# Moving an angle computation into the main loop, and spreading one row by DMA instead of by a matmul

## The chip, the cores and the metric

The kernel runs on one core of one Trainium2 chip. The metric is the device time of one execution in microseconds (us). In what follows TensorE is called PE in the lines of the profile, its weight loads PEld, VectorE is DVE, ScalarE is ACT, GpSimd is POOL and SyncE is SP. An engine name with a q behind it (SPq) is the queue or sequencer of that engine.

## The reference, cut to what matters

```python
x: (8, 3008, 256)                       # float32
X = real(fft(fft(x, axis=1), axis=2))   # (8*3008, 256) rows
g   = X @ w_gate                        # w_gate, w_val: (256, 1536)
val = X @ w_val
out = (silu(g) * val) @ w_out           # w_out: (1536, 256), float32
```

The kernel folds the 256-point transform over the columns into the weights, and does the 3008-point transform with a table of sines and cosines. The rows of one image come in pairs (row k and row M - k) that are a sum and a difference of the same two parts, P and Q. So one set of matmuls serves two rows: "hp" is the result for the plus row, "hm" for the minus row.

## The kernel before

The work runs over 24 tiles of up to 512 row pairs, and each tile over 12 blocks f of 128 hidden columns. One pair (tile, f) is called a unit, so there are 288 units; "unit 2.4" is tile 2, f = 4, and "unit 24" is unit 2.0. A unit has part_a (the plus rows) and, one unit later, part_b (the minus rows, by adding a correction matmul to the same PSUM buffer). Between them stand the output matmuls of the previous tile ("o<-Wo,hp" and "o<-Wo,hm"), four at a time.

The kernel keeps eight PSUM buffers, shared out as 3 + 3 + 2.

```python
psG = tile_pool(name="psG", bufs=3, space=PSUM)   # g
psV = tile_pool(name="psV", bufs=3, space=PSUM)   # v, and e, o of split units
psO = tile_pool(name="psO", bufs=2, space=PSUM)   # outputs
```

From tile 2 on, six of the twelve units of a tile (nine in tiles 21 and 22, none in the last tile) are "split": their value part is not completed in PSUM but as e and o, two PSUM buffers, so that VectorE makes vv from them and GpSimd does the last product. A split unit needs the row d = 0 of Q on all partitions, as "bc". The kernel before makes bc at the first unit of each tile with a matmul against sel (a matrix with ones in its row 0), followed by a ScalarE copy:

```python
SPLIT = (0, 2, 3, 5, 7, 9)
...
def part_a(u):
    ...
    g = psG.tile([P, T], F32, name="g")
    mm(g, Wp, 0, Pt, True, False)
    mm(g, Wq, 0, Qt, False, True)
    if split(u):
        e = psV.tile([P, T], F32, name="v")
        mm(e, Wp, 1, Pt, True, True)
        o = psV.tile([P, T], F32, name="v")
        mm(o, Wm, 1, Qt, True, True)
        sg = ...silu(g)                                             # ScalarE
        stt(es, bc[t], w0[:, f:f + 1], e, mult, add)                # VectorE
        stt(vp, o, -0.5, es, ...); stt(vm, o, 0.5, es, ...)         # VectorE
        nc.gpsimd.tensor_tensor(hts[t][0][:, f], sg, vp, op=mult)   # GpSimd: hp
        return
    v = psV.tile([P, T], F32, name="v")
    ...                                  # two matmuls; ScalarE sg; VectorE hp
def part_b(u):
    ...    # g += Wm.Q (and v += Wm.Q); ScalarE sg; hm on GpSimd (split) or VectorE
...
for i, u in enumerate(units):
    t, f = u
    if f == 0 and split((t, SPLIT[0])):
        ps = psG.tile([P, T], F32, name="g")
        nc.tensor.matmul(ps[:, :w], sel, pq_tiles(t)[1][:, :w], start=True, stop=True)
        bc[t] = bcp.tile([P, T], F32, name="bc")
        nc.scalar.copy(bc[t][:, :w], ps[:, :w])
    for fn in before.pop(i, ()):
        fn()
    run_loads(3)                   # up to three loads of the next image, on the SP queue
    part_a(u)
    if owork:
        owork.run(4)               # four output matmuls of the tile before
    part_b(prev)
    ...
    if owork and not (prev[1] == nF - 1):
        owork.run(4)
    ...                            # fold steps of the next images on GpSimd, transforms on TensorE
```

Before the loop, and while it runs tile 0, the kernel still builds the odd entries 4i + 1 of the sine table. Their angles (four VectorE instructions) stand in front of the loop; their magnitudes, sines and cosines are hung on units 3 to 8 of tile 0 by the table "before". The "fold" of an image is a chain of GpSimd adds (SDf, EOf, Af, then CE and BB) over loaded rows: XA holds rows of one image ("A"), XC rows of two images ("C").

## Time and profile before

| what | value | view |
|---|---|---|
| time | 700.44 us median of 4 runs, 700.24 to 701.84 | the times |
| span of the profiled run, mean granted clock | 698.6 us, 0.987 | cores |
| TensorE, GpSimd, VectorE, ScalarE busy | 97%, 85%, 74%, 62% | part 1 of the page |
| TensorE in the chain that ended last | 83% | part 4 of the page |
| 21 sel matmuls, 21 ScalarE copies | starts 0.216 us apart; 12.3 us | trace; groups |

The page first. Its part 1 gives the busy time of each engine, its part 2 cuts the span into 40 slices of 17.5 us and shows the busy share (and the granted TensorE clock) of each in tenths. Lines of the page of the kernel before:

```profile
PE 679.1 (97%) x4369; PEld 415.5 (59%) x4369; DVE 519.6 (74%) x925; ACT 433.9 (62%) x765; POOL 593.8 (85%) x577
...
PE   7879989999999999999999999999999999999997
...
POOL 7896999899999999999998989998899655658930
PEclk9979999999999999999999999999999999999999
```

TensorE is full from slice 7 (105 us) on; before, the clock falls (the 7 in the third slice). GpSimd is nearly as full from 70 us to about 540 us.

The groups of instructions show what the change takes away. The columns are line, engine, operation, output and input with shapes, count, then busy us and mean ns of one, then the idle time in front. Two lines of the kernel before:

```profile
L857 ACT COPY bc<-g 128x512 f32<-128x512 f32 (+1 forms) x21 | 12.3, 586 | 5.4 <-PE g L854 5.4
...
L854 PE MATMUL g<-Qt,sel 128*128 128x512 bf16 (+1 forms) x21 | 7.9, 378 | 0.0
```

The mean of 378 ns is not what a matmul costs: the ends of matmuls are modelled, and two in a row start 0.216 us apart at 512 columns. That agrees with the Trainium skill, "TensorE: Matmul & The Clock Gate", section "Wait — 56ns, not 53.3ns?", which gives N over 2.4 GHz plus about 2.5 ns, 215.7 ns at 512 columns. I use this spacing below: a wait of TensorE is the distance of two matmul starts less N/2.4 + 2.5 ns.

The start of the loop, from the timeline of the kernel before. The columns are start and length in us, engine, line, operation, output and input, and in brackets the idle time of that engine before it and what ended it:

```profile
27.12 3.00 DVE L305 SCALAR_TENSOR_TENSOR XA<-XA,mM 128x376 f32<-128x376 f32 x4
...
30.28 0.57 ACT L744 ACTIVATE sg<-g 128x480 f32<-128x480 f32 x1 [4.07 <-DMA XC<-in_x_dram]
...
30.90 0.36 PE L754 MATMUL g<-Qt,Wm 128*128 128x480 bf16 x1 [1.68 <-ACT sg L744]
...
39.62 4.67 POOL L152 TENSOR_TENSOR SDf<-XC 64x1024 f32<-64x1024 f32 x2
...
42.56 2.14 DVE L309 TENSOR_SCALAR XA<-XA 128x752 int32<-128x752 int32 x1
...
44.73 0.92 ACT L315 ACTIVATE Tab<-XA,halfpi 128x752 bf16<-128x752 f32 x1 [2.92 <-DVE XA L309]
...
46.16 0.56 PE L754 MATMUL g<-Qt,Wm 128*128 128x480 bf16 x1 [2.95 <-ACT sg L744]
...
47.28 0.75 DVE L309 TENSOR_SCALAR XA<-XA 128x752 int32<-128x752 int32 x1
```

There are two stalls of TensorE. The first silu (30.28) comes only after the four angle instructions of VectorE (27.12 to 30.12), and TensorE waits 1.68 us for it. (The bracket names a DMA.) At unit 7, the magnitude takes 2.14 us where its second half, at 47.28, takes 0.75 us. It overlaps a pair of GpSimd adds (4.67 us together) and ends 0.41 us after them. The Trainium skill, "SBUF — State Buffer", section "Who interferes with whom", says that a VectorE tensor_scalar in a two-port mode and a GpSimd instruction share a port pair, and that the one which issues second is blocked. The cosine and the next silu stand behind the magnitude, and TensorE waits 2.95 us. In the trace the TensorE clock is half for 3.4 us after the first of these stalls and for 10.2 us after the second.

The third stall is at tile 2, where the first folds must be done. From the timeline of the kernel before:

```profile
69.78 4.67 POOL L152 TENSOR_TENSOR SDf<-XA 128x1024 f32<-128x1024 f32 x2 [6.13 <-DMA XC<-in_x_dram]
...
95.39 2.35 POOL L152 TENSOR_TENSOR SDf<-XC 128x1024 f32<-128x1024 f32 x1 [1.32 <-DMA XA<-in_x_dram]
...
103.29 0.38 PE L717 MATMUL v<-Pt,Wp 128*128 128x512 bf16 x1 [2.39 <-DVE vv L736]
```

GpSimd waits 6.13 us for the loads of image 1 (69.78) and 1.32 us for the next ones (95.39). (The brackets name a load of the other buffer; since the adds read XA and XC, I take the waits to be for their own loads.) It then does the products hp and hm of the split units late, VectorE's vv waits for them, and TensorE waits 2.39 us for vv. Half clock follows for 3.4 us.

Last, the first unit of a later tile, 4.0, in the same view of the kernel before:

```profile
145.67 0.57 ACT L762 ACTIVATE sg<-g 128x480 f32<-128x480 f32 x1 [0.47 <-PE g L754]
...
146.11 0.38 PE L854 MATMUL g<-Qt,sel 128*128 128x512 bf16 x1
...
146.27 0.66 DVE L763 TENSOR_TENSOR hm<-sg,v 128x480 bf16<-128x480 f32 x1 [0.39 <-PE o L677]
...
146.75 0.38 PE L717 MATMUL v<-Pt,Wp 128*128 128x512 bf16 x1
...
146.98 0.38 PE L717 MATMUL v<-Qt,Wm 128*128 128x512 bf16 x1
```

The sel matmul is the one at 146.11. The matmul at 146.98 is that of o (v<-Qt,Wm).

### The profile page before, as it was taken

The page shows a single profiled execution, that of the slowest core. Times are in us where ns is not written, and L with a number is a line of the kernel's source. Part 1 is how long each engine was busy: PE and PEld are TensorE (multiplying, and loading weights), DVE is VectorE, ACT ScalarE, POOL GpSimd, SP SyncE. Part 2 cuts the span into 40 slices and gives each one's busy share as a digit, 9 for nine tenths or more (in the row PEclk, how much of TensorE's full clock was granted, in tenths as well). Part 3 has the DMA queues.
Part 4 walks back from the last instruction along what each step waited for, and adds up shares of the span by engine and source line. Part 5 has one row for each costly group of instructions (what it writes and reads, how often), then busy time and mean ns, then how long its engine had stood idle before and what let it go on. Part 6 is the DMA issues. An engine that isn't in the chain of part 4 may idle for free.

```text
span 698.6 us, 13274 instructions
## 1 busy us (share of the span) xinstructions
PE 679.1 (97%) x4369; PEld 415.5 (59%) x4369; DVE 519.6 (74%) x925; ACT 433.9 (62%) x765; POOL 593.8 (85%) x577
## 2 busy tenths in 40 slices
PE   7879989999999999999999999999999999999997
PEld 4335655566565566565665656655666556656676
DVE  8776667777777778677777777777777777788862
ACT  7465655566565666565665666656666566656663
POOL 7896999899999999999998989998899655658930
PEclk9979999999999999999999999999999999999999
DMA  9636353241612412316125111117111011111112
GB/s 216 112 46 132 107 136 93 63 121 44 160 32 65 132 46 71 111 46 160 34 65 138 39 34 43 46 38 152 37 47 46 31 31 46 45 31 46 46 46 69
DMA packets 45567, 52.55 MB, mean 75 GB/s; under 512 B 6290, under 2 KB 33466, under 8 KB 45498
## 3 DMA queue, kind: packets, MB, share of 16 engines
q1 hardware_dynamic: 42314, 49.35, 26.0%
q0 software_dynamic: 3184, 2.36, 2.5%
q8 instruction: 34, 0.56, 0.3%
q14 instruction: 35, 0.29, 0.1%
HBM read 29.39 MB, written 24.65 MB: 77 GB/s over the span
## 4 chain that ended last, share of the span: by engine, by line
PE 83%; DMA 4%; DVE 4%; issue 4%; POOL 2%; ACT 1%; SPq 1%; ACTq 0%; POOLq 0%; DVEq 0%
PE o L677 32%; PE v L717 16%; PE g L717 15%; PE g L754 8%; PE v L754 4%; PE g L566 3%; PE v L566 3%; DVE vv L736 2%; DMA XC<-in_x_dram 2%; DMA XC_107<-in_x_dram 1%; DMA XA<-in_x_dram 1%; POOL hm L759 1%; DVE vv L734 1%; POOL hp L737 1%; PE g L854 1%
## 5 line engine op out<-in xcount | busy, mean ns | idle before, releaser
L737 POOL TENSOR_TENSOR hp<-sgv,vv 128x512 bf16<-128x512 f32 (+1 forms) x132 | 168.2, 1276 | 49.9 <-DVE vv L734 39.0
L759 POOL TENSOR_TENSOR hm<-sgv,vv 128x512 bf16<-128x512 f32 (+1 forms) x132 | 167.7, 1275 | 8.5 <-ACT sgv L758 8.1
L677 PE MATMUL o<-Wo,hm 128*128 128x256 bf16 (+2 forms) x1140 | 170.5, 273 | 0.0
L677 PE MATMUL o<-Wo,hp 128*128 128x256 bf16 (+2 forms) x1140 | 169.6, 273 | 0.0
L677 PEld LDWEIGHTS <-hp 128*128 128x128 bf16 (+2 forms) x1140 | 111.9, 98 | 68.1 <-issue 8.2
L677 PEld LDWEIGHTS <-hm 128*128 128x128 bf16 (+2 forms) x1140 | 112.2, 99 | 65.8 <-issue 6.6
L732 DVE SCALAR_TENSOR_TENSOR es<-bc,w_85,v 128x512 f32<-128x512 f32 (+1 forms) x132 | 98.1, 743 | 53.0 <-PE v L717 52.8
L745 DVE TENSOR_TENSOR hp<-sg,v 128x512 bf16<-128x512 f32 (+2 forms) x156 | 103.7, 665 | 36.7 <-ACT sg L744 35.9
L744 ACT ACTIVATE sg<-g 128x512 f32<-128x512 f32 (+2 forms) x156 | 90.8, 582 | 45.9 <-PE g L717 41.0
L762 ACT ACTIVATE sg<-g 128x512 f32<-128x512 f32 (+2 forms) x156 | 91.1, 584 | 44.4 <-PE g L754 44.2
L763 DVE TENSOR_TENSOR hm<-sg,v 128x512 bf16<-128x512 f32 (+2 forms) x156 | 103.2, 661 | 19.0 <-ACT sg L762 8.9
L754 PE MATMUL g<-Qt,Wm 128*128 128x512 bf16 (+2 forms) x288 | 108.8, 378 | 5.2 <-ACT sg L744 5.1
L717 PE MATMUL v<-Pt,Wp 128*128 128x512 bf16 (+2 forms) x288 | 108.6, 377 | 2.4 <-DVE vv L736 2.4
L758 ACT ACTIVATE sgv<-g 128x512 f32<-128x512 f32 (+1 forms) x132 | 78.9, 598 | 50.1 <-PE g L754 41.3
L717 PE MATMUL g<-Qt,Wq 128*128 128x512 bf16 (+2 forms) x288 | 108.6, 377 | 0.5 <-DVE Qt L579 0.5
L717 PE MATMUL g<-Pt,Wp 128*128 128x512 bf16 (+2 forms) x288 | 108.8, 378 | 0.1
L729 ACT ACTIVATE sgv<-g 128x512 f32<-128x512 f32 (+1 forms) x132 | 78.7, 596 | 45.0 <-PE g L717 35.9
L734 DVE SCALAR_TENSOR_TENSOR vv<-v,es 128x512 f32<-128x512 f32 (+1 forms) x132 | 91.1, 690 | 19.7 <-POOL hp L737 1.7
L736 DVE SCALAR_TENSOR_TENSOR vv<-v,es 128x512 f32<-128x512 f32 (+1 forms) x132 | 89.7, 680 | 6.2 <-POOL hm L759 3.3
L717 PEld LDWEIGHTS <-Wp 128*128 128x128 bf16 x576 | 56.6, 98 | 42.1 <-issue 5.8
L152 POOL TENSOR_TENSOR SDf<-XA 128x1024 f32<-128x1024 f32 x28 | 66.1, 2365 | 8.0 <-DMA XC<-in_x_dram 6.1
L683 ACT COPY ev<-o 128x512 f32<-128x512 f32 x90 | 52.8, 587 | 30.6 <-PE o L677 29.6
(173 smaller groups left out, 742.2 us busy)
## 6 DMA issues: line engine op xcount, KB each, us to landing
out_dram<-ev SPq DMA_DIRECT2D x96, 128.0 KB
XA<-in_x_dram SPq DMA_DIRECT2D x32, 256.0 KB
XA<-in_x_dram SPq DMA_DIRECT2D x112, 64.0 KB
XC<-in_x_dram SPq DMA_DIRECT2D x105, 32.0 KB
XC<-in_x_dram SPq DMA_DIRECT2D x28, 120.0 KB
out_dram<-ev SPq DMA_DIRECT2D x12, 120.0 KB
out_dram<-ev SPq DMA_DIRECT2D x10, 112.0 KB
XA<-in_x_dram SPq DMA_DIRECT2D x1, 1024.0 KB
```

Of the source, the lines that this page charges most:

```text
L677: nc.tensor.matmul(ps[:n, j, :], hts[minus][:, f, c:c + n], Wo[:, f, :], start=(f == 0), stop=(f == nF - 1))
L717: nc.tensor.matmul(ps[:, :w], Wt[:, gv, fs], src[:, :w], start=start, stop=stop, skip_group_check=True)
L732: stt(es[:, :w], bc[t][:, :w], w0[:, f:f + 1], e[:, :w], op0=Alu.mult, op1=Alu.add)
L734: stt(vp[:, :w], o[:, :w], -0.5, es[:, :w], op0=Alu.mult, op1=Alu.add)
L736: stt(vm[:, w - 1::-1], o[:, :w], 0.5, es[:, :w], op0=Alu.mult, op1=Alu.add)
L737: nc.gpsimd.tensor_tensor(hts[t][0][:, f, :w], sg[:, :w], vp[:, :w], op=Alu.mult)
L744: nc.scalar.activation(sg[:, :w], g[:, :w], AF.Silu)
L745: nc.vector.tensor_tensor(hts[t][0][:, f, :w], sg[:, :w], v[:, :w], op=Alu.mult)
L754: nc.tensor.matmul(ps[:, :w], Wm[:, gv, f * P:(f + 1) * P], Qt[:, :w], start=False, stop=True, skip_group_check=True)
L759: nc.gpsimd.tensor_tensor(hts[t][1][:, f, :w], sg[:, :w], v[:, :w], op=Alu.mult)
L762: nc.scalar.activation(sg[:, :w], g[:, :w], AF.Silu)
L763: nc.vector.tensor_tensor(hts[t][1][:, f, w - 1::-1], sg[:, :w], v[:, :w], op=Alu.mult)
```

## The change

The intent is to take the start of the loop off VectorE's four angle instructions, to put VectorE's work for the 4i + 1 entries where it overlaps no large GpSimd add, and to free TensorE and ScalarE of the sel matmul and its copy: two small DMAs write row 0 of the next tile's Q to DRAM and read it back to all partitions, five units before it is needed (two units for tile 3).

```diff
+    mM = const.tile([P, 4], F32, name="mM")        # was in a pool that closes before the loop
-    mm_, mM = col("mm", 4), col("mM", 4)
+    mm_ = col("mm", 4)
...
-    for ch in range(2):
-        angles(rrO[:, ch], kfO, ch, rrO[:, ch].bitcast(I32))    # in front of the loop
...
+    rowd = tc.dram_tile([nT, T], BF16, name="rowd")
...
-    spread(("C", 1), 14, 1, 12)
-    spread(("A", 1), 14, 13, 24)
+    spread(("C", 1), 14, 6, 14)
+    spread(("A", 1), 14, 15, 24)
...
-    before = {1: weight_unit(1, 0), 2: weight_unit(1, 1),
-              3: [lambda: sine(0, ...)], 4: weight_unit(2, 0), 5: [lambda: sine(1, ...)],
-              6: weight_unit(2, 1) + [lambda: cosines(0)], 7: [lambda: cosines(1)],
-              8: [lambda: weigh(NOO, NTAB)], 9: [lambda: value_rows((1, 2))]}
+    raO = SDf...                                    # the magnitudes go to SDf
+    before = {0: angles_o(0), 1: weight_unit(1, 0), 2: weight_unit(1, 1),
+              3: angles_o(1) + cosine_o(0), 4: weight_unit(2, 0) + cosine_o(1),
+              5: weight_unit(2, 1), 7: sine_o(0), 8: sine_o(1),
+              9: [lambda: weigh(NOO, NTAB), lambda: value_rows((1, 2))]}
...
-        if f == 0 and split((t, SPLIT[0])):
-            ps = psG.tile([P, T], F32, name="g")
-            nc.tensor.matmul(ps[:, :w], sel, pq_tiles(t)[1][:, :w], start=True, stop=True)
-            bc[t] = bcp.tile([P, T], F32, name="bc")
-            nc.scalar.copy(bc[t][:, :w], ps[:, :w])
+        if f == (10 if t == 2 else 7) and t + 1 < nT and split((t + 1, SPLIT[0])):
+            bc[t + 1] = bcp.tile([P, T], BF16, name="bc")
+            nc.sync.dma_start(out=rowd[t + 1:t + 2, :w], in_=pq_tiles(t + 1)[1][0:1, :w])
+            nc.sync.dma_start(out=bc[t + 1][:, :w], in_=rowd[t + 1:t + 2, :w].to_broadcast([P, w]))
```

Here angles_o(ch) is the two angle instructions of one half and its magnitude. The table mM had been in a pool whose space the loop's pools take over, so in the kernel before the first silu waited for the last reader of mM; in the changed one mM stays.

More of the change, by code (lines that the diff above doesn't have):

```diff
@@ L362 @@
     nc.vector.memset(Tab[:, :, :, :, NOO - 1:NOO], 0.0)
-    nc.vector.memset(sel[0:1, :], 1.0)
     vts(m2, pcol, scalar1=0.0, scalar2=-2.0, op0=Alu.not_equal, op1=Alu.mult)
@@ L828, in weights, with angles_o, cosine_o, sine_o @@
         transform_w(fc, gv, k, psO.tile([P, T], F32, name="o"))()
-    def cosines(ch):
-        magnitude(rrO[:, ch], rrO[:, ch])
-        cosine(ch, NOO, NTAB, rrO[:, ch])
     def weight_unit(fc, gv):
         return [lambda k=k: weights(fc, gv, k) for k in range(2)]
-    before = {1: weight_unit(1, 0), 2: weight_unit(1, 1),
-              3: [lambda: sine(0, NOO, NTAB, rrO[:, 0])],
-              4: weight_unit(2, 0),
-              5: [lambda: sine(1, NOO, NTAB, rrO[:, 1])],
-              6: weight_unit(2, 1) + [lambda: cosines(0)],
-              7: [lambda: cosines(1)],
-              8: [lambda: weigh(NOO, NTAB)],
-              9: [lambda: value_rows((1, 2))]}
+    raO = SDf.rearrange("p k a d -> p (k a d)")[:, 0:4 * G].rearrange("p (c q n) -> p c q n", c=2, q=2)
+    def angles_o(ch):
+        return [lambda: angles(rrO[:, ch], kfO, ch, rrO[:, ch].bitcast(I32)),
+                lambda: magnitude(raO[:, ch], rrO[:, ch])]
+    def cosine_o(ch):
+        return [lambda: cosine(ch, NOO, NTAB, raO[:, ch])]
+    def sine_o(ch):
+        return [lambda: sine(ch, NOO, NTAB, rrO[:, ch])]
+    before = {0: angles_o(0), 1: weight_unit(1, 0), 2: weight_unit(1, 1), 3: angles_o(1) + cosine_o(0),
+              4: weight_unit(2, 0) + cosine_o(1), 5: weight_unit(2, 1), 7: sine_o(0), 8: sine_o(1),
+              9: [lambda: weigh(NOO, NTAB), lambda: value_rows((1, 2))]}
     loads = []
@@ L850 @@
         t, f = u
-        if f == 0 and split((t, SPLIT[0])):
-            ps = psG.tile([P, T], F32, name="g")
-            w = width(t)
-            nc.tensor.matmul(ps[:, :w], sel, pq_tiles(t)[1][:, :w], start=True, stop=True)
-            bc.pop(t - 2, None)
-            bc[t] = bcp.tile([P, T], F32, name="bc")
-            nc.scalar.copy(bc[t][:, :w], ps[:, :w])
+        if f == (10 if t == 2 else 7) and t + 1 < nT and split((t + 1, SPLIT[0])):
+            bc.pop(t - 1, None)
+            bc[t + 1] = bcp.tile([P, T], BF16, name="bc")
+            w = width(t + 1)
+            nc.sync.dma_start(out=rowd[t + 1:t + 2, :w], in_=pq_tiles(t + 1)[1][0:1, :w])
+            nc.sync.dma_start(out=bc[t + 1][:, :w], in_=rowd[t + 1:t + 2, :w].to_broadcast([P, w]))
         for fn in before.pop(i, ()):
```

## The prediction

> **What bounds it now.** TensorE: 97% busy by the first part of the page, 83% of the chain that ended last. It loses time only early. By the windows it is busy 13.80 of 17.50 us in 34.9–52.4, 17.24 of 20.0 in 87–107, then 99–100% to 600 us. Its longest waits: for sg (2.9 us) and for vv (2.4). The timeline shows three stalls:
>
> - 29.2–30.9: the first sg starts only at 30.28, as it waits for the four angle instructions on VectorE (27.12–30.12), whose mM column lies in the closed pool.
> - 43.2–46.2: the magnitude of 752 elements takes 2.14 us, ending just after GpSimd's 4.67 us SDf pair (the second takes 0.75 us); cosine (0.92) and sg queue behind it.
> - 100.9–103.3: GpSimd is late with hp: it waited for the image loads of the A fold (6.1 us idle, until 69.78), then for the next C loads (until 95.39).
>
> After each stall the clock falls to half: 3.4, 10.2, 3.4 us, so 8.5 us of TensorE work lost where it is the limit. The Trainium skill ("TensorE: Matmul & The Clock Gate", Part 1) has a 3413 ns activity window; the stretches are one and three of these.
>
> **Removed.** 21 sel matmuls (spacing 0.216 us, 4.5 us of TensorE) and 21 ScalarE copies (0.59 us, 12.4 us, but ScalarE is 62% busy and off the path). The first sg no longer waits for VectorE. The second stall's chain disappears.
>
> **Moved.** VectorE's angles and magnitudes (3.0 + 1.5 us unblocked) stay, half in front of hp of unit 0, half in front of unit 3. From 27 us to the value rows of unit 9 VectorE still has about 17 us (hp/hm 0.63 us each, Wp copies 0.62), so it, not TensorE (13.2 us), sets that stage. The first stall shrinks by 0 to 1 us only; the second is replaced by a smaller one at unit 3. The value rows should be reached near 45.5 instead of 50.53; by unit 24 TensorE is about 7 us ahead.
>
> **Given back.** GpSimd does not follow. The A loads can start 5 us earlier, but the last two now stand behind the first output stores: about 67 instead of 69.8. The C loads of the next images come later in the queue, plus about 2 us for the second small DMA waiting for the first: about 93 instead of 95.4. SP issues are almost back to back there. So GpSimd's hp/hm shift by only 2 to 3 us, and the stall at tile 2 grows from 2.4 to about 7 us. Net of the start: about -2.5 us.
>
> **Added.** Two small DMAs per tile, off the path if they land within five units (10.8 us); at tile 3 only two units are left, perhaps 1 us.
>
> **Sum.** -2.5 (start) -4.0 (20 later sel matmuls; GpSimd, 97–99% busy in 140–300, takes a little) = about -6.5: 694 us, range 688.5 to 698.5.
>
> **Signs.** Value rows near 45–46; no 10 us half-clock stretch; A's first SDf near 67, C's near 93; longest TensorE wait at tile 2 for vv, over 4 us in sum, with a half-clock window behind; 99% TensorE after 110 us.
>
> **What would make it wrong.** If the loads land much earlier, GpSimd follows and the gain is 10–13 us. If the SP queue is held up more by the DMA pair, C folds slip and little remains. If GpSimd saturates, the 4 us are lost too.
>
> Faster by over 2%: 0.06; within 2%: 0.92; slower: 0.02.

## The result and the profile after

The changed kernel took 696.59 us (median of 4 runs, 694.98 to 697.36) against 700.44 us before. The ratio is 0.9938 with a 95% interval of 0.9914 to 0.9962: within 2%, and a real gain of a little over half a per cent. Ratios here and below are the mean time of one kernel's fast runs over the mean of the other's fast runs of the same rounds, so they are not quite the ratio of the medians that I quote beside them. The profiled runs have spans of 698.6 us (clock 0.987) and 694.1 us (clock 0.995).

The page of the changed kernel, the same lines:

```profile
PE 672.0 (97%) x4348; PEld 412.0 (59%) x4348; DVE 519.0 (75%) x924; ACT 423.2 (61%) x744; POOL 593.3 (85%) x577
...
PE   7999969999999999999999999999999999999997
...
POOL 8898999899999899999998989998899655658920
PEclk9999989999999999999999999999999999999999
```

TensorE is shown busy for 7.1 us less, the third slice is whole, but slice 6 (87 to 104 us) has fallen from 8 to 6, and the clock dips there instead. Where the time went is seen best by when the first g matmul of a unit starts, read from both traces:

| unit | before | after | difference |
|---|---|---|---|
| 0.0 | 25.87 | 25.85 | 0.0 |
| 0.2 | 33.62 | 31.25 | -2.4 |
| 0.7 | 42.24 | 40.89 | -1.4 |
| 0.9 | 51.01 | 44.07 | -6.9 |
| 1.0 | 59.69 | 51.00 | -8.7 |
| 2.4 | 93.98 | 85.29 | -8.7 |
| 2.7 | 100.31 | 96.84 | -3.5 |
| 3.0 | 118.51 | 114.74 | -3.8 |
| 10.0 | 310.88 | 307.44 | -3.4 |
| 20.0 | 586.62 | 582.80 | -3.8 |
| 22.0 | 640.86 | 636.50 | -4.4 |
| 23.11 | 684.36 | 680.00 | -4.4 |

So three things happened: tile 0 gained 8.7 us; tile 2 took 5.2 us of it back between units 2.4 and 2.7; and over the nineteen tiles from 3.0 to 22.0 the change gained only 0.6 us (522.35 us before, 521.76 us after), although nineteen sel matmuls of 0.216 us, 4.1 us of work, are gone from that stretch.

The start, timeline of the changed kernel:

```profile
27.10 1.12 DVE L306 SCALAR_TENSOR_TENSOR XA<-XA,mM 128x376 f32<-128x376 f32 x2
...
27.28 0.57 ACT L743 ACTIVATE sg<-g 128x480 f32<-128x480 f32 x1 [1.09 <-DMA XC<-in_x_dram]
...
28.25 1.32 DVE L310 TENSOR_SCALAR SDf<-XA 128x752 int32<-128x752 int32 x1
...
30.19 0.36 PE L753 MATMUL v<-Qt,Wm 128*128 128x480 bf16 x1 [0.79 <-DVE hp L744]
...
35.54 0.72 DVE L310 TENSOR_SCALAR SDf<-XA 128x752 int32<-128x752 int32 x1
...
36.29 0.93 ACT L316 ACTIVATE Tab<-SDf,halfpi 128x752 bf16<-128x752 f32 x1 [0.53 <-DVE SDf L310]
...
36.86 0.36 PE L753 MATMUL v<-Qt,Wm 128*128 128x480 bf16 x1 [0.79 <-DVE hp L744]
...
41.52 4.67 POOL L153 TENSOR_TENSOR SDf<-XC 64x1024 f32<-64x1024 f32 x2
...
43.67 0.54 PE L450 MATMUL o<-SDt,XA 128*128 128x1 bf16 x16
```

The first silu starts at 27.28 instead of 30.28. The waits of 1.68 and 2.95 us have become two of 0.79 us, and no half-clock stretch follows either. The large GpSimd pair (41.52) now comes after both magnitudes (1.32 and 0.72 us). The value rows, the matmul group at 43.67, stood at 50.53 before.

Tile 2, timeline of the changed kernel:

```profile
65.93 4.67 POOL L153 TENSOR_TENSOR SDf<-XA 128x1024 f32<-128x1024 f32 x2 [2.48 <-DMA XA<-in_x_dram]
...
88.18 0.38 PE L716 MATMUL g<-Pt,Wp 128*128 128x512 bf16 x1 [0.78 <-ACT sgv L757]
...
90.95 0.38 PE L716 MATMUL v<-Qt,Wm 128*128 128x512 bf16 x1 [1.97 <-DVE vv L735]
...
91.82 2.35 POOL L153 TENSOR_TENSOR SDf<-XC 128x1024 f32<-128x1024 f32 x1 [1.65 <-DMA XA<-in_x_dram]
...
96.07 0.38 PE L753 MATMUL g<-Qt,Wm 128*128 128x512 bf16 x1 [2.13 <-ACT sgv L728]
...
99.69 0.59 PE L716 MATMUL v<-Pt,Wp 128*128 128x512 bf16 x1 [1.79 <-DVE vv L735]
```

TensorE came 8.9 us earlier to tile 2, but GpSimd's folds only 3.9 us (69.78 to 65.93) and 3.6 us (95.39 to 91.82) earlier. TensorE stands for it four times, with up to 2.13 us shown, and half clock follows for 6.8 us. By the spacing of starts, its waits over 0.1 us in units 24 to 33 grew from 4.93 to 10.18 us. These sums, here and below, count the longer spacing under half clock as waiting (without it they are 3.51 and 8.02 us), and leave out the gaps where a matmul record is missing from the trace. The tile gives back what GpSimd did not follow: the difference after it, -3.5 us at unit 2.7, is GpSimd's own.

The chain of waits that ended last shows what GpSimd waited for. Two pieces of it, with start, length and what, of the changed kernel:

```profile
82.62 3.52 DMA XC<-in_x_dram
...
88.89 2.81 DMA XC<-in_x_dram
```

Both are the loads of the next C fold on their way from DRAM; the issues of the SP queue stand between them, the last C load at 89.77.

And a later tile, first unit of tile 4, timeline of the changed kernel:

```profile
142.10 0.57 ACT L761 ACTIVATE sg<-g 128x480 f32<-128x480 f32 x1 [0.47 <-PE g L753]
...
142.70 0.65 DVE L762 TENSOR_TENSOR hm<-sg,v 128x480 bf16<-128x480 f32 x1 [0.39 <-ACT sg L761]
...
142.97 0.38 PE L716 MATMUL v<-Pt,Wp 128*128 128x512 bf16 x1
...
143.41 0.38 PE L716 MATMUL v<-Qt,Wm 128*128 128x512 bf16 x1
```

The last two lines are the matmuls of e and o. They start 0.44 us apart where 0.216 us is the pace. The o matmul starts 0.06 us after hm of line 762 ends, as it did before. There is no bracket behind it: the modelled length of 0.38 us covers the gap. The sum of such waits in front of the o matmul at f = 0, in tiles 3 to 22, is 1.04 us before and 5.14 us after (19 of the 20 times). At f = 3, which is split in tiles 3 to 20, the sums are 4.94 and 4.97 us: there both kernels wait.

### The profile page after: what moved, and what is told of

It reads as the page before. It is cut to its first block, busy times and chain, and to the rows that moved or that the text cites. A ratio compares the mean times of both kernels' runs of the same rounds, so it can differ in the third digit from the quotient of the medians.

```text
span 694.1 us, 13286 instructions
## 1 busy us (share of the span) xinstructions
PE 672.0 (97%) x4348; PEld 412.0 (59%) x4348; DVE 519.0 (75%) x924; ACT 423.2 (61%) x744; POOL 593.3 (85%) x577
## 4 chain that ended last, share of the span: by engine, by line
PE 78%; DVE 6%; DMA 5%; issue 4%; POOL 3%; ACT 2%; SPq 2%; POOLq 0%; DVEq 0%; ACTq 0%
PE o L675 31%; PE v L716 16%; PE g L716 14%; PE g L753 8%; PE v L753 3%; PE g L566 3%; PE v L566 3%; DMA XC<-in_x_dram 3%; DVE vv L735 2%; DVE hm L762 2%; ACT sg L761 2%; POOL hp L736 1%; DMA XC_108<-in_x_dram 1%; DMA XA<-in_x_dram 1%; DVE vv L733 1%
## 5 line engine op out<-in xcount | busy, mean ns | idle before, releaser
L731 DVE SCALAR_TENSOR_TENSOR es<-bc,w_85,v 128x512 f32<-128x512 bf16 (+1 forms) x132 | 98.2, 744 | 48.5 <-PE v L716 48.1
```

Source lines behind the costliest of these rows:

```text
L731: stt(es[:, :w], bc[t][:, :w], w0[:, f:f + 1], e[:, :w], op0=Alu.mult, op1=Alu.add)
```

## The theories

For the 4 us that did not come in tiles 3 to 22:

- **T1.** The o matmul of unit t.0 needs a psV buffer. There are three; the one it takes was last held by the value of unit 10 of the tile before, and VectorE's hm of that unit frees it. That end is set by the chain matmul of part_b, silu, hm, not by what TensorE does meanwhile. The sel matmul stood inside this wait and cost nothing; taking it away only made the wait longer.
- **T2.** GpSimd sets the pace in tiles 2 to 14, where it is 97% busy (184.72 of 190 us between 110 and 300 us, by the windows of the kernel before), and swallowed the gain. This is the prediction's "GpSimd takes a little", made large.
- **T3.** The 4 us were saved, and it was the start that gained nothing.

For the start: the gain is given back at tile 2 because the fold of GpSimd does not move with it, partly for the loads and partly for GpSimd's own order of work (the prediction's account), or because the mM pool alone was the matter.

## The experiments

All twelve results were correct. "Before" is the kernel before, run on the same chip; its median was 701.37, 701.19, 701.45 and 701.16 us in the four calls. "Same" means within 2%; "unclear" means that the interval contains 0.98.

| call | run | built on | median us | ratio to before, 95% interval | class |
|---|---|---|---|---|---|
| 1 | bc_only | before | 700.59 | 0.9991 [0.9955, 1.0028] | same |
| 1 | angles_only | after | 694.84 | 0.9907 [0.9884, 0.9930] | same |
| 1 | sel_filler | after | 695.98 | 0.9922 [0.9900, 0.9944] | same |
| 1 | o_late0 | after | 692.35 | 0.9875 [0.9854, 0.9896] | same |
| 2 | o_late03 | after | 690.96 | 0.9838 [0.9805, 0.9872] | same |
| 2 | loads4 | after | 694.37 | 0.9889 [0.9859, 0.9919] | same |
| 2 | loads4_clate | after | 691.83 (five fast runs) | 0.9867 [0.9827, 0.9908] | same |
| 2 | all3 | after | 688.08 | 0.9807 [0.9777, 0.9836] | unclear |
| 3 | mM_only | before | 699.70 | 0.9982 [0.9950, 1.0015] | same |
| 3 | sel_o_late03 | angles_only | 690.32 | 0.9845 [0.9820, 0.9870] | same |
| 3 | all3_slot | all3 | 685.99 | 0.9791 [0.9759, 0.9823] | unclear |
| 4 | best | all3_slot | 685.01 | 0.9779 [0.9744, 0.9815] | unclear |

For the traces I use three stretches, each from the first g matmul of one unit to that of another: the start (0.0 to 2.0), tile 2 (2.0 to 3.0) and the body (3.0 to 22.0).

| kernel | start | tile 2 | body | half-clock stretches in the body |
|---|---|---|---|---|
| before | 59.59 | 33.05 | 522.35 | none |
| after | 50.71 | 38.18 | 521.76 | none |
| bc_only | 56.35 | 34.00 | 521.76 | none |
| angles_only | 50.94 | 35.49 | 522.38 | none |
| sel_filler | 50.96 | 39.15 | 522.24 | none |
| o_late0 | 50.83 | 38.21 | 517.89 | none |
| o_late03 | 50.74 | 35.69 | 514.86 | none |
| sel_o_late03 | 51.02 | 35.06 | 520.08 | one, 3.4 us |
| mM_only | 57.62 | 33.10 | 522.04 | none |
| loads4 | 50.71 | 35.92 | 521.70 | none |
| all3 | 50.71 | 29.33 | 520.91 | none |
| all3_slot | 50.76 | 32.26 | 522.46 | two, 3.4 us each |
| best | 50.73 | 28.82 | 525.61 | three, 3.4 us each |

A half-clock stretch of 3.4 us costs 1.7 us where TensorE is the limit. It is partly a matter of chance whether one comes, so a single trace is not a time.

### Where did the 4 us go?

**bc_only** is the kernel before with the DMA pair in place of the sel matmul and its copy, and nothing else.

```diff
-        if f == 0 and split((t, SPLIT[0])):
-            ... sel matmul, ScalarE copy
+        if f == (10 if t == 2 else 7) and t + 1 < nT and split((t + 1, SPLIT[0])):
+            ... rowd and bc DMAs
```

> The kernel before with the row spread by the two DMAs alone; angles, cosines and C spread as before. Theory 1 (the slot of the sel matmul is given back to a wait of the second v matmul of unit 0 for its PSUM buffer, which VectorE frees with hm of unit 10): 699.5 to 702 us, ratio 1.00, and in tiles 3 to 22 about 0.2 to 0.26 us of wait in front of that matmul per tile. Theory 2 (GpSimd's pace in tiles 2 to 14 swallowed it): also near 700. Theory 3 (the 4 us of the matmuls were really saved, and the start gained nothing): 696.

Measured: 0.9991, no gain to be seen. In the body 0.6 us are gained, and the wait in front of the o matmul at f = 0 is 5.13 us in 19 waits, as in the changed kernel. The trace's start is 3.2 us shorter than that of before, although nothing was changed there: only 3.4 us of half clock fall in it, behind unit 7, instead of 3.4 and 10.2 us. The first stall is the same (1.68 and 0.33 us). The second is not: the two magnitudes meet other GpSimd instructions and take 1.08 us each instead of 2.14 and 0.75 us, and TensorE waits twice for a silu, 1.74 and 1.80 us, instead of 2.95 and 0.48 us. So some 3 us of the start are a matter of what the magnitudes meet and of where the half clock falls, and the six times of this kernel scatter from 696.4 to 706.5 us. T1 asks for this result. T3 asks for a gain of about 4 us, and falls.

**angles_only** is the changed kernel with the sel matmul and its copy put back.

```diff
-        if f == (10 if t == 2 else 7) and ...:
-            ... rowd and bc DMAs
+        if f == 0 and split((t, SPLIT[0])):
+            ... sel matmul, ScalarE copy
```

> The changed kernel with the sel matmul and the ScalarE copy put back, so only the angle, cosine and C-spread part remains. Theories 1 and 2: nearly the whole gain, 696 to 697.5 us; unit 0 of tile 1 begins 8 to 9 us earlier than before and unit 7 of tile 2 about 3.5 us earlier. Theory 3: 700.

Measured: 0.9907, at least as fast as the changed kernel (0.9938), with the wait at f = 0 back at the level of before. The whole gain is the start's. Tile 2 takes 35.49 us instead of 38.18: with no pair of small DMAs in the SP queue, the C fold begins about 1.2 us earlier (90.7 against 91.82, the traces shifted so that unit 0 starts together). By times the two kernels' intervals overlap, so I take the cost of the pair at tile 2 as seen in traces only.

**sel_filler** is the changed kernel with an added sel matmul at f = 0, whose result nothing reads.

```diff
+        if f == 0 and split((t, SPLIT[0])):
+            ps = psG.tile([P, T], F32, name="g")
+            nc.tensor.matmul(ps[:, :w], sel, pq_tiles(t)[1][:, :w], start=True, stop=True)
```

> The changed kernel with the 21 sel matmuls put back on TensorE into a psG buffer that nobody reads (no ScalarE copy): 4.5 us more of TensorE work. Theory 1: they fill a wait, so the time stays at 696 to 697.5 us. Theory 3, or a TensorE bound in every slot: 700 to 701.

Measured: 0.9922 against the changed kernel's 0.9938; the body is 522.24 against 521.76 us. Work of 4.1 us was put into the body and 0.5 us of it shows. The matmul is free where it stood. T1 asks for this; if TensorE's work were the limit there, it would have cost 4 us. T2 would allow it too, so it is the next run that parts them.

**o_late0** is the changed kernel with the four output matmuls of unit t.0 moved from behind the o matmul to between e and o, so that other work fills the wait.

```diff
+    O_LATE = (0,)
         e = psV.tile([P, T], F32, name="v")
         mm(e, Wp, 1, Pt, True, True)
         o = psV.tile([P, T], F32, name="v")
+        if f in O_LATE and owork:
+            owork.run(4)
         mm(o, Wm, 1, Qt, True, True)
 ...
-        if owork:
+        if owork and not (split(u) and f in O_LATE):
             owork.run(4)
```

> The changed kernel with, in unit 0 of tiles 2 to 22, the four output-projection matmuls that stand behind the second v matmul put in front of it, so that the wait is filled with work. Theory 1: the wait of about 0.26 us per tile goes, 691 to 692.5 us (ratio to the changed kernel 0.993). Theory 2 (GpSimd sets the pace): at most 0.5 us gained, 696.

Measured: 0.9875, 692.35 us. The body is 517.89 us, 3.9 us shorter than that of the changed kernel, and the wait at f = 0 is gone. The first unit of tile 4, timeline of o_late0:

```profile
141.90 0.65 DVE L765 TENSOR_TENSOR hm<-sg,v 128x480 bf16<-128x480 f32 x1 [0.39 <-ACT sg L764]
...
142.17 0.38 PE L717 MATMUL v<-Pt,Wp 128*128 128x512 bf16 x1
...
142.38 0.60 PE L675 MATMUL o<-Wo,hm 128*128 128x256 bf16 x4
...
142.82 0.38 PE L717 MATMUL v<-Qt,Wm 128*128 128x512 bf16 x1
```

The hm at 141.90 still ends 0.17 us after 142.38, but TensorE is busy with the four output matmuls then, and the o matmul follows them at once. No work was taken from any engine, and GpSimd has exactly the same to do. So T2 falls: GpSimd did not stop TensorE from running 3.9 us ahead over these tiles. T1 is shown by three runs that agree: the wait appears with the DMA pair alone, a matmul put into it is free, and filling it gives the 3.9 us.

**o_late03** does the same at f = 3 as well, where both kernels wait.

```diff
-    O_LATE = (0,)
+    O_LATE = (0, 3)
```

> As o_late0, and the same for unit 3 of tiles 2 to 22, where the traces of before and after both show 0.25 to 0.28 us of wait in front of the second v matmul (4.9 us in 18 to 20 tiles). If the wait is VectorE's release of a PSUM buffer and VectorE itself can keep up: 687 to 688.5 us, 5 us under o_late0. If it only moves to the next wait (VectorE or GpSimd paces the tile): 691 to 692.5.

Measured: 690.96 us, 0.9838; I had expected 687 to 688.5 us, so the median missed. The body in the trace is 514.86 us, 6.9 us shorter than that of the changed kernel. The six runs go from 686.16 to 692.17 us, and the profiled run is the fastest of them, at a clock of 0.997. The mechanism holds; its full worth does not come in every run. The six runs stand in the order of their mean granted clocks, from 0.997 (686.16 us) to 0.990 (the three of 691.57 to 692.17 us). My estimate from this difference, 0.7% of 690 us, is 4.8 us, so most of the scatter goes with half clock. Where it falls in the slower runs no trace shows.

**sel_o_late03** is o_late03 with the sel matmul and copy in place of the DMAs, to see whether the removal of sel is worth something once the wait is filled.

```diff
  (angles_only, and)
+    O_LATE = (0, 3)
```

> angles_only (sel matmul and ScalarE copy kept, no small DMAs) with the reordering of o_late03. If the sel matmul was free only because it filled the wait, it costs its 0.216 us per tile once the wait is gone: from unit 0 of tile 3 to unit 0 of tile 22 about 4.1 us longer than in o_late03 (514.9 us there), and 1 us of that is won back at tile 2, where no DMA pair holds the loads up: 692 to 694 us. If it stays free: 515 us from tile 3 to 22 and 688.5 to 690.5.

Measured: 690.32 us, 0.9845, against 0.9838: not to be told apart by times, and inside the 688.5 to 690.5 us that I had expected if the matmul stayed free. In the trace the body is 520.08 us against 514.86 us, of which at most 1.7 us is a half-clock stretch; the rest, 3.5 us, is near the 4.1 us of the nineteen matmuls. The fastest runs are 689.45 and 686.16 us. That the matmul costs its 0.2 us as soon as the wait holds other work is what T1 says, but only the trace bears it out here.

### What became of the gain at the start?

**mM_only** is the kernel before with mM kept in a pool that stays open, one line of the change.

```diff
+    mM = const.tile([P, 4], F32, name="mM")
-    mm_, mM = col("mm", 4), col("mM", 4)
+    mm_ = col("mm", 4)
```

> The kernel before with only the column mM moved to the permanent pool, so that the first sg no longer waits for the angles; angles, magnitudes and cosines stay where they were. The prediction's view (VectorE, not the first sg, sets the stage): hp of unit 0 still stands behind the four angle instructions, so unit 2 begins at most 1 us earlier, the 2.9 us stall of unit 7 stays, and the time is 699.5 to 701.5 us. The rival (the tie of the first sg was the cause of the early loss): unit 2 begins 2 us earlier and no half-clock stretch follows, 697 to 698.5.

Measured: 0.9982, no gain, as expected for the time. In the trace the first silu no longer waits for the angles (it starts at 28.06, the angles at 27.88), and unit 2 begins 5.92 us after unit 0, against 7.75 us before and 5.41 us after: 1.8 us earlier, where I had expected 1 us at most. The trace of bc_only, which has the stall of before but by chance no half clock behind it, has 6.95 us. So the shorter stall is worth 1.0 us and the other 0.8 us is half clock that did not come. The stall at unit 7 stays, 2.9 us with 10.2 us of half clock, so the start is still 57.6 us long; what brings it to 50.7 us is the rest of the change to tile 0. That this is the magnitudes moved away from the GpSimd pair fits the waits; no run moves them alone, and chance has a part in the 10.2 us, as bc_only shows.

**loads4** lets the loop issue four loads for each unit instead of three.

```diff
-        run_loads(3)
+        run_loads(4)
```

> The changed kernel with four image loads queued per unit instead of three, so that all loads of the A fold stand before the first output stores and the C loads come earlier too. If GpSimd's late hp and hm at tile 2 are due to the loads, as predicted: A's first SDf at about 63.5 (GpSimd's own end of the C fold) instead of 65.9, no GpSimd wait before C's SDf, so unit 8 of tile 2 about 4 us earlier, 692 to 693.5 us. If the loads are not what binds there: 696 to 697.

Measured: 694.37 us, 0.9889; I had expected 692 to 693.5 us, so the median missed, and the interval still overlaps that of the changed kernel a little. In the trace the A fold begins at 63.8 instead of 65.93 and the C fold at 88.8 instead of 91.82 (shifted in the same way), and TensorE's waits in units 24 to 33 fall from 10.18 to 7.61 us. Tile 2 is 2.3 us shorter. By this trace the loads, which the SP queue issues one behind the other, hold part of the gain.

**loads4_clate** also begins the C fold of images 2 and 3 five units later, behind more of the products of tile 2.

```diff
-    lo = 25
+    lo = 30
```

> loads4, and the C fold of the next image pair begun at unit 30 instead of 25, so that GpSimd works off the hp and hm of units 24 to 29 first. GpSimd still ends the A fold only about 6 us after TensorE reaches unit 24. Expected: the waits of units 24 to 33, 10 us with the half clock in the changed kernel, shrink to 1 to 4 us, 689 to 691 us. If the A fold alone binds, as loads4: 692 to 693.5.

Measured: of six runs one, the profiled one, was slow (767.65 us at a clock of 0.851). The median of the other five is 691.83 us, above the 689 to 691 us that I had expected; their ratio is 0.9867, with the interval 0.9827 to 0.9908. I use no trace of it. The point is above that of loads4 in gain, but the intervals overlap.

**all3** is loads4_clate with O_LATE = (0, 3).

> loads4_clate and o_late03 together. If the two losses are independent their gains add: 680 to 683 us (ratio to before about 0.972). If GpSimd becomes the limit once TensorE no longer waits (it is 97 to 99 per cent busy from 140 to 300 us): 684 to 688, with TensorE waits for vv or sgv all through tiles 3 to 14.

Measured: 688.08 us, 0.9807, so the gains do not simply add (that would have been 680 to 683 us). Tile 2 takes 29.33 us instead of 38.18, the waits in units 24 to 33 are down to 1.43 us, and no half-clock stretch comes after the start. This points to GpSimd's place in the queue of work as what gave the 5 us back at tile 2: with the loads earlier and the C fold behind the products, TensorE keeps its lead. But the body is 520.91 us, 6 us longer than that of o_late03, all of it in tiles 3 to 5. In tile 3 TensorE comes earlier than the inputs: it waits 2.1 us for es of the first split unit, whose bc the DMA pair brings late (rowd issued at 104.51, bc at 106.15, es at 109.25). The other 4 us are mostly waits for vv in tile 4 and one of 1.9 us in tile 5 for GpSimd's hp, which o_late03 does not have. So once TensorE is this far ahead, GpSimd does hold it up, which T2 had claimed of the changed kernel.

**all3_slot** takes the transform that makes tile 3's inputs two units earlier, and with it the DMA pair.

```diff
-    slot[(1, 0)] += 5
+    slot[(1, 0)] += 3
-        if f == (10 if t == 2 else 7) and ...
+        if f == (8 if t == 2 else 7) and ...
```

> all3 with the transform of the second image begun two units earlier (unit 31), so that the row of tile 3 starts its DMAs two units earlier. In all3 the second unit of tile 3 waits 2.1 us for es, which waits for that row. Expected: that wait goes, 685.5 to 687 us median, ratio to before 0.976 to 0.98. If GpSimd's lag takes it up: as all3, 688.

Measured: 685.99 us, 0.9791. The wait for bc at tile 3 falls from 2.1 to 0.49 us; in return tile 2 waits more again, 4.26 us in units 24 to 33.

**best** has, in addition, only three split units in tile 2 (f = 5, 7, 9), which gives GpSimd six products fewer while it is late.

```diff
-        return 2 <= u[0] < nT - 1 and u[1] in (SPLIT if u[0] < t_end else SPLIT_END)
+        return 2 <= u[0] < nT - 1 and u[1] in (SPLIT[3:] if u[0] == 2 else SPLIT if u[0] < t_end else SPLIT_END)
-        if ... split((t + 1, SPLIT[0])):
+        if ... split((t + 1, SPLIT[3])):
```

> all3_slot with only three split units in tile 2 (5, 7 and 9) instead of six, so that GpSimd, still at the A fold, owes TensorE six products less there. Three more matmuls of 0.216 us on TensorE, against 4.3 us of waits in units 24 to 33 and about 3 to 4 us in tiles 4 and 5 of all3_slot, which are GpSimd's backlog. If GpSimd's backlog is the cause of those waits: unit 24 to 33 waits under 1 us, 680 to 683.5 us, ratio to before about 0.972. If not: 685.5 to 687.

Measured: 685.01 us median, 683.04 to 689.76, 0.9779. I had expected 680 to 683.5 us; that missed. It is the fastest version and beats both kernels: about 16 us below the kernel before, where the changed kernel is 4 us below it; the intervals 0.9744 to 0.9815 and 0.9914 to 0.9962 do not meet. Against all3_slot (0.9759 to 0.9823) it is not told apart. What was missed is seen above all at tile 3, timeline of best:

```profile
104.91 0.23 SPq L861 DMA_DIRECT2D rowd<-Qt  x1
...
106.93 0.34 SPq L862 DMA_DIRECT2D bc<-rowd  x1
...
109.88 0.71 DVE L734 SCALAR_TENSOR_TENSOR es<-bc,w,v 128x480 f32<-128x480 bf16 x1 [4.45 <-DMA bc<-rowd]
110.64 0.56 PE L717 MATMUL v<-Pt,Wp 128*128 128x480 bf16 x1 [3.40 <-DVE es L734]
```

Tile 2 hardly waits any more (0.27 us in units 24 to 33), so tile 3 comes sooner, and VectorE's es there waits 4.45 us for bc. TensorE waits 3.40 us, and half clock follows. The pair takes 4.97 us from its first issue to its first reader (104.91 to 109.88). The wait of 1.9 us for GpSimd's hp in tile 5 stays too, and three half-clock stretches fall in the body.

## Why the prediction was right or wrong, point by point

The prediction said 694.0 us, 688.5 to 698.5, most likely within 2%; the result is 696.59 us and within 2%. That the sum came out near is in good part luck: the gain at the start was forecast 1.3 us too small and the gain of the body 3.4 us too large, and the two errors partly cancel inside a range of 10 us.

- **"-4.0 (20 later sel matmuls; GpSimd ... takes a little)": this is the step that failed.** The body gained 0.6 us. The matmul stood in a wait for a PSUM buffer that VectorE frees, so its removal lengthened the wait (1.04 to 5.14 us at f = 0) and not the lead. It is shown by bc_only, sel_filler and o_late0. GpSimd took nothing to speak of: o_late0 gained 3.9 us with the same GpSimd work. The mistake was to cost the matmul by its spacing and to take "TensorE 99% busy" for "TensorE is the limit at this point". The page could not show the wait, and I had not looked at what the next matmul started after.
- **"about -2.5 us" for the start: the mechanism was right, the size off.** It measured -3.8 us at unit 3.0. The lead of TensorE at tile 2 was predicted as 7 us and was 8.9, of which about 3 us are loss that another trace with the old start (bc_only) did not have either; GpSimd's shift as 2 to 3 us and was 3.6 to 3.9 (folds at 65.93 and 91.82, predicted near 67 and 93).
- **"The first stall shrinks by 0 to 1 us only": wrong in size.** Unit 2 began 2.4 us earlier. Of this, 1.5 us is the stall itself (unit 2 begins 5.41 us after unit 0, in bc_only 6.95 us) and 0.8 us the half clock behind it, which I had not counted as going with the stall.
- **"The second is replaced by a smaller one at unit 3": right.** 0.79 us at 36.86 in place of 2.95 us, and the half-clock stretch of 10.2 us is gone. The value rows came at 43.67, even before the predicted 45 to 46.
- **"The stall at tile 2 grows from 2.4 to about 7 us": right.** The changed kernel's waits there, which the view of waits shows, add up to 6.7 us (3.8 for vv, 2.1 and 0.8 for sgv), and half clock follows, as said. (The longest single one is for sgv, and vv stays just under the 4 us of the forecast.) That loads are a part of its cause is shown by the trace of loads4. That the rest is GpSimd's backlog fits all3 and best, each of which changes several things at once; I call it supported rather than shown.
- **"Perhaps 1 us" for the DMA pair of tile 3:** in the changed kernel es waited only 0.20 us for bc (rowd issued at 111.59, es at 115.80). What the pair costs instead is the SP queue in tile 2, about 1.2 us of the C fold by the traces. In all3 and best, however, the pair of tile 3 becomes a wait of 2.1 and 3.4 us for TensorE.
- **"99% TensorE after 110 us": it is so, and says little.** It was so before as well. Summed over that stretch, the spacing of starts then exceeded the pace by about 22 us, of which 7 us stand in front of o matmuls and most of the rest in the transforms, where I did not separate waits from weight loads.
- "If GpSimd saturates, the 4 us are lost too" named the right loss and the wrong cause.

The clock, which the prediction drew on, behaves as the Trainium skill says in "TensorE: Matmul & The Clock Gate", Part 1: the stretches come in lengths of 3.4, 6.8 and 10.2 us, one to three windows of 3413 ns. The page also calls the window free-running and the effect run-variable. The scatter of runs of one kernel here is in line with that: the six runs of the best version fall into three near 683.3 us at clocks of 0.997 to 1.0 and three of 686.5 to 689.8 us at 0.992 to 0.997. No run here shows where a window begins.

## What to carry to other kernels

Before counting a removed instruction as time saved, find what the next instruction of its engine starts right after: if that is the end of another engine's work (here VectorE freeing one of three PSUM buffers, 0.05 us before), the removed one stood in a wait and was free. An engine shown as 99% busy can still hide such waits, so compare the spacing of its starts with its pace, and test with a filler that does nothing and with a reorder that fills the gap. And a lead won early lasts only if every engine that feeds the next stage moves with it; look at when the loads and folds for that stage begin, not at the engine that was freed.

## What the Trainium skill lacked or had wrong

- "TensorE: Matmul & The Clock Gate", Part 1, gives at least one idle window as the condition for half rate, and tells further down of a kernel whose many short idle times brought half rate, without saying how much idle time is enough. Here half clock followed windows in which TensorE was partly busy, 1.41, 1.23 and 1.03 of 3.41 us by the traces, and did not follow one with 1.76 of 3.41 us. In the run sel_o_late03 it followed even a stretch with 2.97 of 3.42 us busy (312.95 to 316.37), which held transform matmuls with short or one-column weights. What the gate counts as activity stays open.
- "DMA: Bandwidth & Descriptors", section "Anatomy of one DMA — SWDGE (gpsimd) path", gives a fixed cost of about 2.0 us for that path, most of it the write receipt of the target memory. No page gives the time of a store to DRAM and a broadcast back on the hardware queue of SP. Here the pair took 4.2 us (111.59 to 115.80, changed kernel) to 5.0 us (104.91 to 109.88, best) from the first issue to the first reader, and the second DMA held the SP queue, waiting for the first, 23.0 us in 21 waits, up to 1.9 us.
- "Perfetto Trace Analysis" warns that matmul busy time is a bad metric, because matmuls are pipelined. Neither it nor another page that I found gives the size of a wait that this hides. Here matmuls are drawn 0.38 us long at a pace of 0.216 us, so the 0.22 us that TensorE waits in front of an o matmul for a PSUM buffer show no idle time; they sum to 5.14 us at f = 0 (tiles 3 to 22) and 4.97 us at f = 3 (tiles 3 to 20).
